# Joint first layers of a two-MoE kernel: fixed PSUM bank pairs, additions issued earlier, an earlier set of inner sums, and a third raw weight buffer

## The chip, the cores and the metric

The kernel runs on one core of a Trainium2 chip. Its time is in device microseconds (us), the median over timed executions; beside them stands one execution under the hardware profiler, from which every row below comes. Matrix products run on TensorE (PE in the rows; PEld is its weight load), element work on VectorE (DVE), ScalarE (ACT) and GpSimd (POOL); the sync engine (SP) issues the loads of the weights.

## The reference

An attention with a score threshold makes x (1152 x 512), which then passes through two mixtures of experts. Every expert is a dense two-layer network over all rows.

```python
def _moe_ref(x, w_gate, w1, w2):           # 8 experts
    ...                                    # P: gate, balanced 8 times
    for e in range(E):
        h = np.maximum(x @ w1[e], 0.0)     # 512 -> 1024
        ye = h @ w2[e]                     # 1024 -> 512
        out += P[:, e:e + 1] * ye

def _moe2_ref(x, domain_probs, w1, w2):    # 4 experts, the same form
    ...
    for e in range(E):
        h = np.maximum(x @ w1[e], 0.0)
        out += p[:, e:e + 1] * (h @ w2[e])
```

## The kernel before

**Work and stages.** After the attention (with two experts' share of rows computed behind it) the experts are run in 22 halves, each one half of an expert's 1024 inner columns. A half has a first layer (x times w1, then relu) and a second layer (times w2, added to `acc`). Every fp32 product is three fp32r products of a high and a low part: of a weight `wh` (a cast on ScalarE) and `wl` (a subtraction on GpSimd), of a hidden value `hs` high (a relu on ScalarE) and `hs` low (a scalar_tensor_tensor on VectorE, called a low part below).

**Two kinds of half.** The first layer is a Winograd form of Strassen's scheme: 7 products numbered `u` = 1 to 7 in place of 8, with sums of x and of the weights' quarters made beforehand. Six halves run it for one chunk of 576 rows at a time (`layer1`, then `layer2` of that chunk; chunk c is the first or second 576 rows). The other 16 (`TWO`: halves 3 to 12 and 16 to 21) are joint: `layer1_two` takes both chunks together, and for u = 2 and u = 7 applies the scheme once more inside; then one `layer2` goes over all 9 tiles of rows. A joint half has 162 first-layer matmuls of 288 columns (L1076) and 108 second-layer ones of 512 columns (L1279, 12 for each tile).

**Order in a joint first layer.** `ROW` is the order of TensorE's groups by hand. "a1" to "a7" are the inner products of u = 2, "b1" to "b7" those of u = 7 (3 matmuls each); "101" is u = 1, chunk 0, half of the columns 1 (6 matmuls). Copies to SBUF follow on ScalarE at once (`s`, `u`, `w` 576 wide, `A`, `B`, `C` 288 wide, tag `inner`); additions, relus and low parts are put on VectorE's and ScalarE's queues by `after(k, op)`, k slots of `ROW` later, and `done(k, ...)` is a relu after k slots and its low part one slot later. Each engine runs its queue in this order.

**Banks.** PSUM is one tile of 8 banks. `A01` are two pairs, of chunk 0 and chunk 1, for u = 1, 6, 5, 3; `X` and `Y` are pairs for the inner products of a, then again for those of b, and from there for u = 4. `ps.pair()` takes the pair that came free first, `bank()` the bank that came free first, in the program's order; `give` returns one behind the instruction that reads it last (the low part, or the addition into `acc`). The layer after waits on the chip for that reader.

**Weights.** `cook1` and `cook2` prepare units of w1 and w2: raw tiles are loaded by SP, `cook1` makes sums of quarters on GpSimd (`ws`, `wx`, in-place `raw`), and each unit is a cast and a subtraction. `tick()` places one unit at a time between the rest of the work. Of w2 two raw buffers exist (`raw2`).

**Inner sums of x.** `within_x` makes the sums of x that a and b need (24 additions or subtractions of 288 columns and low parts on VectorE, 8 casts on ScalarE) before the first joint half of each run of joint halves. It is started by `start_within()` in halves 2 and 15, and `tick` spreads it over the second layer that follows, up to 6 steps a tile.

Of the kernel before, what the change touches and what calls it, by code (L numbers as in the profile page):

```python
# [20 lines left out]
P = 128  # L21
# [9 lines left out]
def attention_two_moe_kernel(ctx, tc, qP, kP, qT, kT, vp, tau, wg, w1, w1s, w2, dp, m2w1s, m2w2, out):  # L31
# [601 lines left out]
    class Psum:  # L633
# [7 lines left out]
            self.of[id(t)] = t, (k,)  # L641
            return t

        def pair(self):
            j = min((j for j in range(4) if 2 * j in self.free and 2 * j + 1 in self.free),
                    key=lambda j: max(self.free.index(2 * j), self.free.index(2 * j + 1)))
            for k in (2 * j, 2 * j + 1):
                self.free.remove(k)
            t = self.all[:, 2 * j:2 * j + 2]
            self.of[id(t)] = t, (2 * j, 2 * j + 1)  # L650
            return t

        def give(self, t):
# [20 lines left out]
    def cook1():  # L674
# [7 lines left out]
        for i, hv in enumerate(halves):  # L682
# [20 lines left out]
                return x, clock[0] + LAG  # L703

            if i in TWO:
                yield 0, ready
                x2 = within(a12)
                yield from unit(a12, ready)
                yield from unit(*x2)
# [7 lines left out]
            yield 0, ready  # L717
            G.tensor_tensor(a21, a11, a21, op=ALU.subtract)  # L718
            s3 = a21, clock[0] + LAG
            yield from unit(*s2)  # L720
            if i in TWO:
                yield from unit(*s1)
                x7 = within(a21)
                yield from unit(*s3)
                yield from unit(*x7)
            else:
                yield from unit(*s3)
                yield from unit(*s1)
            yield 0, ready
            G.tensor_tensor(a12, a12, s2[0], op=ALU.subtract)  # L730
            yield from unit(a12, clock[0] + LAG)
            yield from unit(a22, ready)

    def cook2(w2p):
        raw = []
        todo2 = [(hv, k) for hv in halves for k in ORDER]
        for i in range(len(todo2)):
            while len(raw) < 2 and todo2:
                hv, k = todo2.pop(0)
                raw.append((w2p.tile([P, DM], F32, tag="raw2", name="raw", bufs=2), clock[0] + LAND))  # L740
                nc.sync.dma_start(raw[-1][0], hv["w2"][hv["e"], :, hv["hf"] * HF + k])
            yield i, raw[0][1]
            hi = w2p.tile([P, DM], F32R, tag="w2h", name="wh", bufs=NB2)
            lo = w2p.tile([P, DM], F32R, tag="w2l", name="wl", bufs=NB2)
            split(A, G, hi, lo, raw.pop(0)[0])
            units[1].append((hi, lo))
# [305 lines left out]
    def layer1_two(i):  # L1052
# [83 lines left out]
            after(at, go)  # L1136

        v, ps = {}, banks.pool
        A01 = [ps.pair(), ps.pair()]
        X = Y = None  # L1140
        for slot in ROW:
            if slot[0] in "ab":
                u, j = {"a": 2, "b": 7}[slot[0]], int(slot[1])
                if j == 1:
                    X, Y = ps.pair(), ps.pair()
                m = {1: X[:, 0], 6: X[:, 0], 5: X[:, 0], 3: X[:, 0], 2: Y[:, 0], 7: Y[:, 1], 4: Y[:, 1]}[j][:, :HS]
                inside(u, j, m, j in (1, 2, 7))
                if j in (1, 6, 5):
                    copy("ABC"[(1, 6, 5).index(j)], m, "inner", 3, False)
                if j == 2:  # L1150
                    after(1, lambda m=m: add(m, v["A"], m))
                if j == 5 and u == 2:
                    def far(X=X, Y=Y):
                        add(X[:, 1, :HS], v["C"], Y[:, 1, :HS])
                    after(1, far)
                if j == 5 and u == 7:
                    def far(Y=Y):
                        add(v["C"], v["C"], Y[:, 1, :HS])
                    after(1, far)
                    after(2, lambda: add(v["w1"][:, 1], v["w1"][:, 1], v["C"]))  # L1160
                    after(3, lambda: add(v["u1"][:, 1], v["u1"][:, 1], v["C"]))
                if j == 3 and u == 2:
                    after(1, lambda X=X: add(cols(X), v["s1"], cols(X)))
                    done(2, cols(X), 1, 0, 0, (X,))
                if j == 3 and u == 7:
                    after(1, lambda m=m: add(v["w1"][:, 0], v["w1"][:, 0], m))
                    done(2, v["w1"], 1, 1, 2)
                    rest(6, 1, 1)
                if j == 4:
                    after(1, lambda m=m: add(m, v["B"], m))  # L1170
                    if u == 2:
                        after(2, lambda Y=Y: add(cols(Y), v["s0"], cols(Y)))
                        done(3, cols(Y), 0, 0, 0, (Y,))
                    else:
                        after(1, lambda Y=Y: add(v["w0"], v["w0"], cols(Y)))
                        done(2, v["w0"], 0, 1, 2)
                        rest(6, 0, 1)
                if n[0] % 2:
                    tick()
# [79 lines left out]
    def layer2(i, c):  # L1259
# [10 lines left out]
            if c == hv["chunks"][-1]:  # L1270
                ts.insert(2, 8)
        for t in ts:
            py = bank()
            hs, o = (tail, 0) if t == 8 else (hv["side"][t // 4][t % 4 // 2], P * (t % 2))
            n = 0
            for j, k in enumerate(ORDER):
# [28 lines left out]
    for i, hv in enumerate(halves):  # L1305
# [4 lines left out]
        for c in hv["chunks"]:  # L1310
            layer1(i, c)
            if i == 0:
                while behind:
                    next(behind[0], None) or behind.pop(0)
                begin(0, sums(0), 2)
            if (i == 2 or i == turn + 2) and c == hv["chunks"][-1]:
                start_within()
            layer2(i, c)

# [53 lines left out]
```

## Time and profile before

| what | value |
|---|---|
| three timed runs | 1379.47, 1380.01, 1380.37 us (median 1380.01) |
| the profiled execution | 1379.62 us, span 1377.8 us from first to last instruction |
| TensorE busy | 1321.3 us of the span, mean granted clock 0.991 |
| VectorE, ScalarE, GpSimd busy | 734.2, 598.4, 814.8 us |
| one joint half (511.65 to 559.85 us) | 48.20 us |

The median lies 0.39 us above the profiled execution. TensorE is busy nearly always, so what matters is the few places where it stood still, which engine ended that, and what that engine was doing before. A busy TensorE is not one at full clock: the granted clock of a stretch says which of its two levels (1.2 and 2.4 GHz) it had.

### The profile page before, as it was taken

The page shows a single profiled execution, that of the slowest core. Times are in us where ns is not written, and L with a number is a line of the kernel's source. Part 1 is how long each engine was busy: PE and PEld are TensorE (multiplying, and loading weights), DVE is VectorE, ACT ScalarE, POOL GpSimd, SP SyncE. Part 2 cuts the span into 40 slices and gives each one's busy share as a digit, 9 for nine tenths or more (in the row PEclk, how much of TensorE's full clock was granted, in tenths as well). Part 3 has the DMA queues.
Part 4 walks back from the last instruction along what each step waited for, and adds up shares of the span by engine and source line. Part 5 has one row for each costly group of instructions (what it writes and reads, how often), then busy time and mean ns, then how long its engine had stood idle before and what let it go on. Part 6 is the DMA issues. An engine that isn't in the chain of part 4 may idle for free.

```text
span 1377.8 us, 20664 instructions
## 1 busy us (share of the span) xinstructions
PE 1321.3 (96%) x7681; PEld 1159.6 (84%) x7681; DVE 734.2 (53%) x1478; ACT 598.4 (43%) x1220; POOL 814.8 (59%) x997
## 2 busy tenths in 40 slices
PE   7998999999998999999999999999999899999998
PEld 4687988898787888898888888888788788888887
DVE  5799888266757543453454345344335645435524
ACT  6887786223433443243234324324533424333431
POOL 6886875252855755674575566455854467556540
PEclk9999999999999999999999999999999999999999
DMA  4542320010220121021011101111110101101101
GB/s 153 157 122 68 107 90 9 24 47 16 77 69 16 47 62 48 15 62 62 16 47 62 52 11 62 61 46 32 46 35 28 62 3 60 62 24 39 62 8 69
DMA packets 42051, 73.54 MB, mean 53 GB/s; under 512 B 5088, under 2 KB 10336, under 8 KB 41952
## 3 DMA queue, kind: packets, MB, share of 16 engines
q1 hardware_dynamic: 41664, 71.96, 16.8%
q8 instruction: 60, 0.98, 0.3%
q10 hardware_dynamic: 288, 0.28, 0.1%
q14 instruction: 39, 0.32, 0.1%
HBM read 69.86 MB, written 2.36 MB: 52 GB/s over the span
## 4 chain that ended last, share of the span: by engine, by line
PE 69%; DVE 12%; ACT 8%; POOL 5%; DMA 3%; issue 2%; DVEq 0%; POOLq 0%; ACTq 0%
PE mm L1279 35%; PE mm L1076 14%; PE mm L979 6%; PE mm L501 4%; PE mm L473 3%; POOL wl L77 2%; DMA raw<-in_w 2%; ACT wh L72 2%; DVE hs L1122 2%; PE pv L349 2%; PE sc L272 1%; DVE ex L296 1%; ACT hs L1118 1%; DVE acc L1287 1%; DVE st L277 1%
## 5 line engine op out<-in xcount | busy, mean ns | idle before, releaser
L77 POOL TENSOR_TENSOR wl<-raw,wh 128x512 fp32r<-128x512 f32 x198 | 261.7, 1328 | 336.1 <-ACT wh L72 333.6
L1279 PE MATMUL mm<-wh,hs 128*128 128x512 f32 x1344 | 432.7, 395 | 2.5 <-DVE hs L952 2.4
L1279 PEld LDWEIGHTS mm<-wh,hs 128*128 128x128 f32 x1344 | 252.4, 188 | 65.5 <-DVE hs L952 6.6
L1279 PE MATMUL mm<-wl,hs 128*128 128x512 f32 x672 | 265.3, 395 | 1.6 <-POOL wl L77 1.6
L1287 DVE SCALAR_TENSOR_TENSOR acc<-mm,p,acc 128x512 f32<-128x512 f32 x181 | 133.8, 748 | 244.8 <-PE mm L1279 244.6
L72 ACT CAST wh<-raw 128x512 fp32r<-128x512 f32 x198 | 122.4, 622 | 73.5 <-POOL raw L718 33.1
L1279 PEld LDWEIGHTS mm<-wl,hs 128*128 128x128 f32 x672 | 126.3, 188 | 30.2 <-POOL wl L77 2.3
L1076 PE MATMUL mm<-xh,wl 128*128 128x288 f32 x432 | 99.8, 304 | 18.5 <-DVE acc L1287 18.4
L1122 DVE SCALAR_TENSOR_TENSOR hs<-mm,hs 128x576 fp32r<-128x576 f32 x96 | 72.5, 755 | 68.8 <-ACT hs L1118 65.8
L1118 ACT ACTIVATE hs<-mm 128x576 fp32r<-128x576 f32 x96 | 62.4, 650 | 82.3 <-DVE mm L1115 81.5
L1076 PE MATMUL mm<-xl,wh 128*128 128x288 f32 x432 | 97.5, 298 | 0.0
L1076 PE MATMUL mm<-xh,wh 128*128 128x288 f32 x432 | 97.0, 297 | 0.0
L1076 PEld LDWEIGHTS mm<-xh,wl 128*128 128x128 f32 x432 | 72.0, 192 | 23.5 <-DVE acc L1287 22.8
L1112 ACT COPY A<-mm 128x288 f32<-128x288 f32 x32 | 13.1, 408 | 171.5 <-PE mm L1076 171.5
L1076 PE MATMUL mm<-xth,wl 128*128 128x288 f32 x304 | 71.1, 302 | 9.7 <-DVE hs L1122 9.3
L1134 POOL TENSOR_SCALAR ht<-hs 128x128 fp32r<-128x128 f32 x128 | 44.3, 359 | 48.8 <-ACT hs L1118 32.9
L1076 PEld LDWEIGHTS mm<-xl,wh 128*128 128x128 f32 x432 | 72.1, 192 | 0.7
L1076 PEld LDWEIGHTS mm<-xh,wh 128*128 128x128 f32 x432 | 72.0, 192 | 0.0
L306 POOL TENSOR_SCALAR ex<-ex,st 128x576 f32<-128x576 f32 x72 | 54.1, 752 | 26.6 <-DVE st L304 23.6
L1076 PE MATMUL mm<-xth,wh 128*128 128x288 f32 x304 | 68.9, 295 | 0.0
L1076 PE MATMUL mm<-xtl,wh 128*128 128x288 f32 x304 | 68.8, 295 | 0.0
L296 DVE SCALAR_TENSOR_TENSOR ex<-sc,st,ex 128x576 f32<-128x576 f32 x72 | 58.5, 813 | 14.8 <-ACT ex L292 11.0
(220 smaller groups left out, 3002.0 us busy)
## 6 DMA issues: line engine op xcount, KB each, us to landing
raw<-in_w SPq DMA_DIRECT2D x88, 256.0 KB, 2.9
raw<-in_w1s SPq DMA_DIRECT2D x56, 256.0 KB, 3.7
raw<-in_m2w1s SPq DMA_DIRECT2D x32, 256.0 KB, 3.5
raw<-in_m2w SPq DMA_DIRECT2D x32, 256.0 KB, 2.9
kr<-in_kT SPq DMA_DIRECT2D x22, 288.0 KB, 2.8
vr<-in_vp SPq DMA_DIRECT2D x24, 160.0 KB, 2.4
qr<-in_qT SPq DMA_DIRECT2D x8, 288.0 KB, 2.8
out_y<-acc SPq DMA_DIRECT2D x8, 256.0 KB, 2.0
```

The lines of the kernel that those rows point to most:

```text
L72: A.copy(hi, src)
L77: el.tensor_tensor(lo, src, f(hi), op=ALU.subtract)
L296: V.scalar_tensor_tensor(ex, u["sc"][:, :, :HS], st[:, 2:3], ex, op0=ALU.is_ge, op1=ALU.mult, accum_out=st[:, 3:4])
L306: G.tensor_scalar(exf, exf, st[:, 5:6], 1.0, op0=ALU.mult, op1=ALU.mult)
L501: T.matmul(py, lhsT=x, rhs=a, start=i == 0, stop=i == 3 * FT - 1)
L979: T.matmul(m, lhsT=w[:, (2 * g + kt) * P:(2 * g + kt + 1) * P], rhs=operand(u, kt, lo), start=first and j == 0, stop=j == len(ops) - 1, sk ...
L1076: T.matmul(m, lhsT=w, rhs=x, start=first and j == 0, stop=last and j == len(ops) - 1, skip_group_check=True)
L1118: A.activation(sides[c][s][0][:, k:k + 2], src, AF.Relu)
L1122: V.scalar_tensor_tensor(hl, src, 0.0, f(hh), op0=ALU.max, op1=ALU.subtract)
L1134: G.tensor_scalar(tail[j][:, :, q:q + 32], f(sides[c][s][j][:, :, 2 * P:]), 1.0, 1.0, op0=ALU.mult, op1=ALU.mult)
L1279: T.matmul(py, lhsT=hs[x][:, k, o:o + P], rhs=w, start=n == 0, stop=n == 3 * HF - 1)
L1287: V.scalar_tensor_tensor(acc[t], py, s, acc[t], op0=ALU.mult, op1=ALU.add)
```

## The change

It touches the joint halves (their banks, their order on VectorE and ScalarE), the order of `cook1` in all halves, the number of raw w2 buffers, and the place where `within_x` starts.

- Banks: `A01` is always banks 0, 1 and 2, 3; `X` is 4, 5 and `Y` 6, 7, both for a and for b. The second layer of a joint half uses banks 2 and 3 by turns in place of all eight.
- `after` and `done` have smaller k: an addition goes on the queue in the slot of the product that it waits for.
- `inner` copies have 2 buffers in place of 3, raw w2 tiles 3 in place of 2.
- `cook1` makes the subtraction for its second to last unit (`s4`) before the units s2, s1, s3, and in joint halves the sums `x7` as well; the first sums `x2` get a start LAG later.
- `start_within()` stands behind the first layer of the half's first chunk, not of its last.

```diff
-        def pair(self):
-            j = min((j for j in range(4) if 2 * j in self.free and 2 * j + 1 in self.free),
-                    key=lambda j: max(self.free.index(2 * j), self.free.index(2 * j + 1)))
-            for k in (2 * j, 2 * j + 1):
+        def take(self, *ks):
+            for k in ks:
                 self.free.remove(k)
...
             if i in TWO:
-                yield 0, ready
+                yield 0, ready + LAG
                 x2 = within(a12)
...
-            yield from unit(*s2)
-            if i in TWO:
-                yield from unit(*s1)
-                x7 = within(a21)
-                yield from unit(*s3)
-                yield from unit(*x7)
-            else:
-                yield from unit(*s3)
-                yield from unit(*s1)
             yield 0, ready
             G.tensor_tensor(a12, a12, s2[0], op=ALU.subtract)
-            yield from unit(a12, clock[0] + LAG)
+            s4 = a12, clock[0] + LAG
+            if i in TWO:
+                yield 0, ready
+                x7 = within(a21)
+                rest = s2, s1, s3, x7, s4
+            else:
+                rest = s2, s3, s1, s4
+            for src in rest:
+                yield from unit(*src)
...
-            while len(raw) < 2 and todo2:
+            while len(raw) < 3 and todo2:
...
-        A01 = [ps.pair(), ps.pair()]
+        A01 = [ps.take(0, 1), ps.take(2, 3)]
...
-                    X, Y = ps.pair(), ps.pair()
+                    X, Y = ps.take(4, 5), ps.take(6, 7)
...
-                    copy("ABC"[(1, 6, 5).index(j)], m, "inner", 3, False)
+                    copy("ABC"[(1, 6, 5).index(j)], m, "inner", 2, False)
...
                 if j == 3 and u == 2:
-                    after(1, lambda X=X: add(cols(X), v["s1"], cols(X)))
-                    done(2, cols(X), 1, 0, 0, (X,))
+                    after(0, lambda X=X: add(cols(X), v["s1"], cols(X)))
+                    done(1, cols(X), 1, 0, 0, (X,))
                 if j == 3 and u == 7:
-                    after(1, lambda m=m: add(v["w1"][:, 0], v["w1"][:, 0], m))
-                    done(2, v["w1"], 1, 1, 2)
+                    after(0, lambda m=m: add(v["w1"][:, 0], v["w1"][:, 0], m))
+                    done(1, v["w1"], 1, 1, 2)
                     rest(6, 1, 1)
                 if j == 4:
-                    after(1, lambda m=m: add(m, v["B"], m))
+                    after(0, lambda m=m: add(m, v["B"], m))
                     if u == 2:
-                        after(2, lambda Y=Y: add(cols(Y), v["s0"], cols(Y)))
-                        done(3, cols(Y), 0, 0, 0, (Y,))
+                        after(0, lambda Y=Y: add(cols(Y), v["s0"], cols(Y)))
+                        done(1, cols(Y), 0, 0, 0, (Y,))
                     else:
-                        after(1, lambda Y=Y: add(v["w0"], v["w0"], cols(Y)))
-                        done(2, v["w0"], 0, 1, 2)
+                        after(0, lambda Y=Y: add(v["w0"], v["w0"], cols(Y)))
+                        done(1, v["w0"], 0, 1, 2)
                         rest(6, 0, 1)
...
-            py = bank()
+            py = banks.pool.take(2 + ts.index(t) % 2) if i in TWO else bank()
...
-            if (i == 2 or i == turn + 2) and c == hv["chunks"][-1]:
+            if (i == 2 or i == turn + 2) and c == hv["chunks"][0]:
                 start_within()
```

The order on ScalarE in the middle of a joint first layer, from the copy `s` of chunk 0 to the copy `w` of chunk 0, before:

```order
L1112 COPY s_5781<-mm 128x576
L1112 COPY C<-mm 128x288
L72 CAST wh<-raw 128x512
L1112 COPY s_5809<-mm 128x576
L72 CAST wh<-raw 128x512
L1112 COPY u_5837<-mm 128x576
L72 CAST wh<-raw 128x512
L1118 ACTIVATE hs<-mm 128x576
L1112 COPY u_5859<-mm 128x576
L72 CAST wh<-raw 128x512
L1118 ACTIVATE hs<-mm 128x576
L1112 COPY w_5887<-mm 128x576
```

and of the change:

```order
L1109 COPY s_5783<-mm 128x576
L72 CAST wh<-raw 128x512
L1109 COPY C<-mm 128x288
L72 CAST wh<-raw 128x512
L1109 COPY s_5818<-mm 128x576
L1115 ACTIVATE hs<-mm 128x576
L1109 COPY u_5842<-mm 128x576
L72 CAST wh<-raw 128x512
L1115 ACTIVATE hs<-mm 128x576
L1109 COPY u_5863<-mm 128x576
L72 CAST wh<-raw 128x512
L1109 COPY w_5889<-mm 128x576
```

The fourth cast of w2 (the second cast of the rows, before as of the change) now stands ahead of the second `s`, and the relu of `X` follows that copy directly, where a cast, a copy and a cast stood between them.

The order on VectorE from the addition of `C` of b to the last low part of the w's, near the end of the joint first layer (`w_5887` is chunk 0, `w_5915` chunk 1), before:

```order
L1115 TENSOR_TENSOR C<-C,mm 128x288
L1115 TENSOR_TENSOR w_5915<-w_5915,C 128x288
L1122 SCALAR_TENSOR_TENSOR hs<-mm,hs 128x576
L1115 TENSOR_TENSOR u_5859<-u_5859,C 128x288
L1115 TENSOR_TENSOR w_5915<-w_5915,mm 128x288
L1115 TENSOR_TENSOR mm<-B,mm 128x288
L1115 TENSOR_TENSOR w_5887<-w_5887,mm 128x576
L1122 SCALAR_TENSOR_TENSOR hs<-w_5915,hs 128x576
L1122 SCALAR_TENSOR_TENSOR hs<-mm,hs 128x576
L1122 SCALAR_TENSOR_TENSOR hs<-w_5887,hs 128x576
```

and of the change (`w_5889` is chunk 0, `w_5917` chunk 1):

```order
L1112 TENSOR_TENSOR C<-C,mm 128x288
L1112 TENSOR_TENSOR w_5917<-w_5917,C 128x288
L1119 SCALAR_TENSOR_TENSOR hs<-mm,hs 128x576
L1112 TENSOR_TENSOR u_5863<-u_5863,C 128x288
L1112 TENSOR_TENSOR w_5917<-w_5917,mm 128x288
L1112 TENSOR_TENSOR mm<-B,mm 128x288
L1112 TENSOR_TENSOR w_5889<-w_5889,mm 128x576
L1119 SCALAR_TENSOR_TENSOR hs<-w_5917,hs 128x576
L1119 SCALAR_TENSOR_TENSOR hs<-w_5889,hs 128x576
L1119 SCALAR_TENSOR_TENSOR hs<-mm,hs 128x576
```

The second `hs<-mm`, the low part that gives back the pair of chunk 1 (now banks 2 and 3), has moved from second to last place among the three low parts.

## Rows read from the trace of the kernel before

**Rows 1.** The page, busy time of each engine with its share of the span.

```profile
PE 1321.3 (96%) x7681; PEld 1159.6 (84%) x7681; DVE 734.2 (53%) x1478; ACT 598.4 (43%) x1220; POOL 814.8 (59%) x997
```

**Rows 2.** TensorE's waits: waiting line, releaser, us in total, times, longest.

```profile
PE mm L1076 <- DVE acc L1287: 18.4, 16, 6.1
PE mm L1076 <- DVE hs L1122: 9.3, 16, 1.0
...
PE mm L1279 <- POOL wl L77: 1.6, 2, 1.4
```

**Rows 3.** Windows, second and first layer: us; busy PE, PEld, DVE, ACT, POOL; granted clock.

```profile
511.65:536.80 25.15, 25.15 (x110) 20.33 (x110) 9.99 (x15) 4.09 (x7) 13.93 (x20) 1.00 0.00 1
536.80:559.85 23.05, 22.03 (x163) 21.56 (x162) 11.16 (x18) 13.55 (x26) 14.75 (x14) 1.00 0.31 92
```

**Rows 4.** Timeline of TensorE in one joint first layer: start, us, idle before.

```profile
488.36 0.29 PE L1076 MATMUL mm<-xh,wl 128*128 128x288 f32 x1
...
489.36 0.40 PE L1076 MATMUL mm<-xh,wl 128*128 128x288 f32 x1 [0.45 <-DVE acc L1287]
...
500.77 0.42 PE L1076 MATMUL mm<-xh,wh 128*128 128x288 f32 x2
...
501.81 0.40 PE L1076 MATMUL mm<-xth,wl 128*128 128x288 f32 x1 [0.62 <-DVE hs L1122]
...
511.49 0.40 PE L1279 MATMUL mm<-wh,hs 128*128 128x512 f32 x1
```

**Rows 5.** The chain of waits that ends at 501.81.

```profile
493.58 2.83 DMA raw<-in_w
...
500.24 0.66 ACT hs L1118
...
501.00 0.77 DVE hs L1122
```

**Rows 6.** Timeline of VectorE from b's `C` to the next second layer.

```profile
505.74 0.46 DVE L1115 TENSOR_TENSOR C<-C,mm 128x288 f32<-128x288 f32 x1 [2.71 <-ACT C L1112]
...
509.60 1.57 DVE L1122 SCALAR_TENSOR_TENSOR hs<-w,hs 128x576 fp32r<-128x576 f32 x1
511.10 0.74 DVE L1122 SCALAR_TENSOR_TENSOR hs<-mm,hs 128x576 fp32r<-128x576 f32 x1
511.76 1.18 DVE L1122 SCALAR_TENSOR_TENSOR hs<-w,hs 128x576 fp32r<-128x576 f32 x1
...
517.16 1.40 DVE L1287 SCALAR_TENSOR_TENSOR acc<-mm,p,acc 128x512 f32<-128x512 f32 x2
```

**Rows 7.** Timeline of GpSimd in the same stretch.

```profile
503.13 0.46 POOL L702 TENSOR_TENSOR wx<-raw 128x128 f32<-128x128 f32 x1 [2.05 <-DMA raw<-in_w1s]
...
510.64 1.70 POOL L679 TENSOR_TENSOR ws<-ws,raw 128x512 f32<-128x512 f32 x1
```

**Rows 8.** Timeline of VectorE, inner sums of x, in two places.

```profile
421.54 3.85 DVE L1034 TENSOR_TENSOR sums<-xh,xl 128x288 f32<-128x288 f32 x4
...
433.44 1.55 DVE L1034 TENSOR_TENSOR sums<-xth,xtl 128x288 f32<-128x288 f32 x4
```

**Rows 9.** Windows: the wait of the first joint half, and its first 12 matmuls.

```profile
433.40:439.56 6.16, 0.04 (x1) 0.00 (x1) 6.09 (x16) 1.53 (x4) 0.00 (x0) 0.68 0.00 0
439.56:442.56 3.00, 3.00 (x12) 3.00 (x13) 1.07 (x2) 0.92 (x2) 0.88 (x1) 0.51 0.00 0
```

**Rows 10.** Timeline of TensorE, the same wait in half 16.

```profile
1083.81 0.61 PE L1076 MATMUL mm<-xh,wl 128*128 128x288 f32 x1 [5.99 <-DVE acc L1287]
```

**Rows 11.** Timeline of VectorE, then of GpSimd, half 2's first second layer.

```profile
398.25 0.46 DVE L952 SCALAR_TENSOR_TENSOR hs<-mm,hs 128x288 fp32r<-128x288 f32 x1 [0.48 <-ACT hs L951]
...
402.25 0.75 DVE L1287 SCALAR_TENSOR_TENSOR acc<-mm,p,acc 128x512 f32<-128x512 f32 x1 [2.04 <-PE mm L1279]
...
410.25 0.46 DVE L994 TENSOR_TENSOR mm<-s,mm 128x288 f32<-128x288 f32 x1 [1.69 <-PE mm L979]
...
410.38 1.29 POOL L77 TENSOR_TENSOR wl<-raw,wh 128x512 fp32r<-128x512 f32 x1 [11.30 <-ACT wh L72]
```

More of the change, by code (lines that the diff above doesn't have):

```diff
@@ L642, in tile @@
             return t
-        def pair(self):
-            j = min((j for j in range(4) if 2 * j in self.free and 2 * j + 1 in self.free),
-                    key=lambda j: max(self.free.index(2 * j), self.free.index(2 * j + 1)))
-            for k in (2 * j, 2 * j + 1):
+        def take(self, *ks):
+            for k in ks:
                 self.free.remove(k)
-            t = self.all[:, 2 * j:2 * j + 2]
-            self.of[id(t)] = t, (2 * j, 2 * j + 1)
+            t = self.all[:, ks[0]] if len(ks) == 1 else self.all[:, ks[0]:ks[1] + 1]
+            self.of[id(t)] = t, ks
             return t
@@ L737, in cook2 @@
         for i in range(len(todo2)):
-            while len(raw) < 2 and todo2:
+            while len(raw) < 3 and todo2:
                 hv, k = todo2.pop(0)
-                raw.append((w2p.tile([P, DM], F32, tag="raw2", name="raw", bufs=2), clock[0] + LAND))
+                raw.append((w2p.tile([P, DM], F32, tag="raw2", name="raw", bufs=3), clock[0] + LAND))
                 nc.sync.dma_start(raw[-1][0], hv["w2"][hv["e"], :, hv["hf"] * HF + k])
@@ L1148, in layer1_two @@
                 if j in (1, 6, 5):
-                    copy("ABC"[(1, 6, 5).index(j)], m, "inner", 3, False)
+                    copy("ABC"[(1, 6, 5).index(j)], m, "inner", 2, False)
                 if j == 2:
-                    after(1, lambda m=m: add(m, v["A"], m))
+                    after(0, lambda m=m: add(m, v["A"], m))
                 if j == 5 and u == 2:
@@ L1154, in far @@
                         add(X[:, 1, :HS], v["C"], Y[:, 1, :HS])
-                    after(1, far)
+                    after(0, far)
                 if j == 5 and u == 7:
@@ L1158, in far @@
                         add(v["C"], v["C"], Y[:, 1, :HS])
-                    after(1, far)
+                    after(0, far)
                     after(2, lambda: add(v["w1"][:, 1], v["w1"][:, 1], v["C"]))
```

## The prediction

> **What bounds the kernel now.** I read the busy times first, then TensorE's waits, then the joint halves stage by stage, then the timeline around each wait. TensorE is busy 1321.3 of 1377.8 us [rows 1], so only the 56 us in which it stands still, and what they entail, can be won. The list of its waits shows where half of them lie: in the joint first layers it waits 18.4 us for an `acc` addition (16 times) and 9.3 us for a low part (16 times) [rows 2]. Sixteen is the number of joint halves: each has one wait of either kind.
>
> A joint half repeats in 48.20 us [rows 3]. Its second layer runs without a gap: 9 tiles in 25.15 us, 2.79 us a tile. Its first layer takes 23.05 us, while 162 matmuls at 0.133 us (the last 72 take 501.81 to 511.49 us [rows 4]) need 21.55. The missing 1.5 us are two stalls:
>
> - Stall A, at "a2". The 3 matmuls of "a1" start at 488.36 and need 0.40 us, the next starts only at 489.36 [rows 4]: 0.60 us lost, and 0.1 more because the first matmul behind a pause takes 0.40 where 0.29 is usual. It waits for the `acc` addition of the last tile, whose bank had become `Y`.
> - Stall B, at "b2". After 500.77 the two matmuls need 0.27 us, the next starts at 501.81: 0.77 lost, and again 0.1. The profile shows 0.62 of it as idle [rows 4]. The bank is a's `Y`, given back by a low part at 501.00 [rows 5]. Followed back, that low part stands behind a relu at 500.24, this behind an addition, and that behind the low part of `X`; and all of it behind a cast on ScalarE that waited for a load of raw w2, 493.58 + 2.83 = 496.41 us [rows 5].
>
> In the first joint half of each run stall A is of another size: 6.12 and 5.99 us [rows 9, 10], because VectorE was busy 6.09 of 6.16 us [rows 9], with the inner sums and the `acc` additions queued behind them. Then comes a second price: the first 12 matmuls take 3.00 us at a granted clock of 0.51, the 1.2 GHz level, in place of 12 x 0.133 = 1.6 [rows 9].
>
> **What each part changes, and its price.**
>
> 1. *Stall A, 14 usual ones.* "a2" now writes bank 6. The second layer writes only 2 and 3, and 6 was given back at its beginning. The idle time of the 14 is 18.4 - 6.12 - 5.99 = 6.3 us [rows 2, 9, 10]; each costs 0.6 + 0.1 where 0.45 is shown, so 14 x 0.27 = 3.8 more. Gain 10.1. Bank 2 is needed next at "110", 3.2 us into the layer, long after the last tile's addition (0.75 us, [rows 11]).
>
> 2. *Stall B, 16.* With three raw buffers the load for the fourth w2 cast starts behind the first subtraction in place of the second, about 2.9 us into the layer, and lands at 5.75 (duration of [rows 5]). The relu of `X` follows its addition at once, and `Y`'s addition goes ahead of `X`'s low part. Step by step from the layer's start (a group of 6 takes 0.8 us, results are seen 0.2 later): copy of the second `s` 6.3 to 6.9, addition of `X` to 7.7, relu to 8.4, a copy and a cast to 9.5, relu of `Y` to 10.2, its low part to 10.95. "b2" wants the bank at 12.0: 1 us to spare. The cover is this slack; without it the stall is back. Gain 9.3 + 16 x 0.27 = 13.6.
>
> 3. *Inner sums.* They move to the second layer of the first chunk, two stages earlier. There VectorE idles 2.04 us of each 2.79 us tile [rows 11] and GpSimd 11.30 us in one piece [rows 11]. That matters: four sums took 3.85 us while GpSimd worked and 1.55 while it rested [rows 8]. At the second pace 8 additions, 8 subtractions and 8 low parts, 24 x 0.4, are 10 us, with four `acc` additions of 0.75 almost 13, from 398.7 (the first layer's last low part) to 411.4 us. VectorE's next work began at 410.25 [rows 11], so it starts 1.2 us late. Queued behind are that first layer's additions and, on ScalarE behind 8 casts, its copies `s`; TensorE wants the first `s` read 3.2 us into that layer, and by this count it is, with 1 us to spare. I take no cost; the bound is the old pace throughout, 24 x 0.96 = 23 us in place of 10, some 5 to 10 us too late for that layer each time, of which a later stall would bring back up to 5. Gain (6.12 + 5.99) + 2 x 0.16 + 2 x 1.4 of slow clock = 15.2, at least 5.
>
> 4. *A new wait at the second layer's start.* The second layer begins in bank 2, which chunk 1's low part gives back, and this now stands last of three low parts on VectorE. Before, b's `C` went in 5.75 us ahead of the second layer (505.74 against 511.49), and the chain from there ran without a pause to 512.94, 1.45 us behind that start [rows 6]. Its length is partly GpSimd's doing: low parts with an SBUF source took 1.57 and 1.18 us, one from PSUM 0.74 [rows 6], while GpSimd worked from 503.13 to 512.3 [rows 7]. With the new order GpSimd has only the `wx` sums until then: the cast for the next subtraction stands behind the relu of chunk 1 on ScalarE, and the `ws` sums behind the tails. So I price the chain without contention: the two additions with `C` as before and, behind its relu, chunk 0's low part from 4.7 to 4.0 us ahead of the start, three additions of 0.4 to 2.8, `w0` (576 wide) to 2.1, the low part of `w1` to 1.4, that of `w0` behind its relu from 1.3 to 0.6, and chunk 1's with its 0.74 [rows 6] until 0.16 behind the start. The price is 0.2 + 0.1 = 0.3 us a half, 16 x 0.3 = 4.8. The bounds: nothing, if it is 0.2 faster; and, if the chain keeps its old length with the two low parts exchanged, 512.94 + 0.74 - 511.49 = 2.2 us, with 0.1 for the restart 16 x 2.3 = 37. I take the lower one, since the work that made the old rows long is queued later.
>
> 5. *Two banks in the second layer.* A tile needs 2.79 us, its addition 0.75 [rows 3, 11], so with turns a bank is free 2 us before it is wanted. The exception is the first: its addition came at 517.16 [rows 6], while the third tile would want its bank at 511.49 + 2 x 2.79 = 517.07, and the addition ends near 517.9. In the new order the chain of step 4 is about 1.2 us shorter, the addition ends near 516.6, and the tile wants the bank at 517.3. Cost nothing, bound 16 x 0.8 = 13.
>
>    The Trainium skill, page "Perfetto Trace Analysis" (section "Matmul Optimizations"), speaks against this edit: it asks that all 8 banks be put to use. By it the second layer would lose time, which the last rival prices; by the rows the sum stays as it is, since 0.75 is less than 2.79.
>
> 6. *The rest.* The third buffer places one cast of the first half earlier, where TensorE waits 1.6 us for GpSimd's subtraction [rows 2]; between 0 and 3 with its restarts, I take 1. The order in `cook1` moves one subtraction of about 1.3 us ahead of the units; in a second layer GpSimd is busy 13.93 of 25.15 us [rows 3], which leaves room. Two `inner` buffers: each copy comes after the addition that read its buffer two copies ago. Nothing for both.
>
> Sum: 10.1 + 13.6 + 15.2 + 1 - 4.8 = 35.1 us. The profiled execution took 1379.62, so 1344.5; the median of the runs is 0.4 above its own profile, which gives **1345**.
>
> **Rivals.**
>
> - *The low parts stay slow* (chance 0.2). GpSimd still works in the last 3 us of the first layer, for example because the loads for `wx` land late (they landed at 503.13 [rows 7], 8.4 us before the end). Then step 4 costs between 1 and 2 us a half, or step 5 its 0.8: 1354 to 1370. For it: [rows 6] as they are. Against: the order on ScalarE.
> - *The sums only move their stall* (0.08). If GpSimd's work falls on them, TensorE waits at the copies of half 2 and half 15: up to 10 us less gain, 1349 to 1355.
> - *The new wait takes everything* (0.03 slower, 0.04 no change). The place is bank 2 at the start of the second layer. Step 4 without its price gains 39.9 us, so from 39.9 / 16 = 2.5 us a half the kernel is slower. The old chain with the low parts exchanged gives 2.3, which is 1376.5; 0.2 us more contention and it is no gain. It needs GpSimd as busy as in [rows 7], with all three low parts at 1.57.
> - *The wait of B stays* (0.04), if the load of the fourth raw tile lands over 1 us later than I reckon: 13.6 less, 1358.
> - *Two banks bind every tile* (0.01). If no addition overlapped the next tiles, each of the 144 joint tiles would wait 0.8 us, 115 us in all: 1460. It would need additions 2 us late, tile after tile; [rows 11] show them in 0.75 with 2.04 of rest. The skill's rule on banks, named in step 5, is this case.
>
> **How the numbers follow.** My forecast, 1340 to 1349, has the remaining 0.6. The rivals of 1349 to 1362 take in some 0.2 more; below 1340 lies only the case that step 4 costs nothing. So the range is 1338 to 1362. Changes under 0.2% (2.8 us) can't be told from none. Faster 0.92, within it 0.04, slower 0.04.
>
> **What would show it.** Right: a joint half of 46.9 to 47.1 us; no wait of TensorE for `acc` in the joint first layers; 16 short waits at L1276 for the last low part; the sums uncontended, near 0.39 us each; a granted clock of 1.0 in the first matmuls of halves 3 and 16. Wrong: idle time over 0.5 us before the first or the third second-layer tile, low parts from SBUF above 1 us, or TensorE waiting at L976 in halves 2 and 15.

## The result, and the profile after

The changed kernel took **1343.45 us** (median of 4 runs, 1342.15 to 1344.37), the kernel before in the same session 1379.74 (1378.57 to 1380.37): ratio 0.9737, 95% interval 0.972 to 0.9754. Forecast: 1345, range 1338 to 1362. Line numbers behind the weights' code moved up by three: L1076 is now L1073, L1279 is L1276, L1122 is L1119.

The page of the changed kernel, busy time (beside [rows 1]):

```profile
PE 1311.2 (98%) x7681; PEld 1156.2 (86%) x7681; DVE 706.0 (53%) x1478; ACT 600.9 (45%) x1220; POOL 788.4 (59%) x997
```

The span fell from 1377.8 to 1341.1 us. TensorE's waits, of which [rows 2] showed 18.4 us for `acc` and 9.3 for a low part:

```profile
PE mm L976 <- ACT u L983: 2.1, 2, 1.9
...
PE mm L976 <- ACT w L983: 1.4, 2, 0.8
...
PE mm L976 <- ACT s L983: 0.9, 1, 0.9
...
PE mm L1276 <- DVE hs L1119: 0.3, 1, 0.3
```

Both large lines are gone. In the joint halves the list names one wait, 0.3 us. The waits for copies of ScalarE in the first layers of other halves (L976) have grown to 4.4 us; before there was one, 0.7 us for a `w`. A joint half, second and first layer (windows, beside [rows 3]), and the first matmuls of halves 3 and 16 (beside [rows 9]):

```profile
500.64:525.84 25.20, 25.20 (x109) 20.39 (x110) 8.71 (x12) 4.25 (x8) 17.31 (x23) 1.00 0.00 1
525.84:547.56 21.72, 21.69 (x164) 21.45 (x162) 11.12 (x20) 13.67 (x26) 9.84 (x11) 1.00 0.31 97
432.02:433.62 1.60, 1.60 (x14) 1.59 (x13) 1.22 (x2) 0.92 (x2) 0.01 (x1) 1.00 0.00 0
1055.66:1057.26 1.60, 1.60 (x14) 1.59 (x13) 1.22 (x2) 0.92 (x2) 0.01 (x1) 1.00 0.00 0
```

46.92 us in place of 48.20; and the first joint halves start at a granted clock of 1.00 where 0.51 stood.

Where the 36.7 us of span came from, read from the first matmul of each stretch (for half 3 before, 433.27, the turn of its first matmul, which stalled):

| stretch | before | after | gained | forecast |
|---|---|---|---|---|
| up to half 0 (code that the change doesn't touch) | 331.17 | 329.65 | 1.5 | 0 |
| halves 0 to 2 | 102.10 | 102.37 | -0.3 | 1 |
| half 3 and half 16, the first joint ones | 55.09, 55.42 | 46.91, 46.90 | 16.7 | 16.3 |
| 14 other joint halves | 434.79, 245.22 | 422.65, 238.54 | 18.8 | 17.8 |
| halves 13 to 15 | 154.01 | 154.08 | -0.1 | 0 |

The forecasts of the joint halves are the terms of the text: 15.2 + 2 x (0.85 - 0.3) for the first ones, 14 x (0.72 + 0.85 - 0.3) for the others. The first row is scatter: in the profiles below half 0 begins anywhere from 329.73 to 331.53.

**The new wait.** TensorE at the second layer's start, and VectorE before it (timelines of the changed kernel):

```profile
500.19 0.42 PE L1073 MATMUL mm<-xth,wh 128*128 128x288 f32 x2
500.64 0.50 PE L1276 MATMUL mm<-wh,hs 128*128 128x512 f32 x1
500.98 0.39 PE L1276 MATMUL mm<-wl,hs 128*128 128x512 f32 x1
```

```profile
494.71 0.46 DVE L1112 TENSOR_TENSOR C<-C,mm 128x288 f32<-128x288 f32 x1 [2.71 <-ACT C L1109]
...
498.32 1.59 DVE L1119 SCALAR_TENSOR_TENSOR hs<-w,hs 128x576 fp32r<-128x576 f32 x2
499.84 0.75 DVE L1119 SCALAR_TENSOR_TENSOR hs<-mm,hs 128x576 fp32r<-128x576 f32 x1
```

Two matmuls from 500.19 need 0.27, so the next was due at 500.46 and came at 500.64, when the low part that gives bank 2 back ends (499.84 + 0.75 = 500.59); and it is followed after 0.34 where 0.23 is usual. 0.18 + 0.1 = 0.28 us: the forecast said 0.3. The low parts of the `w` took 0.8 us each, not the 1.57 and 1.18 of [rows 6], and GpSimd stood still beside them, for 7.27 us up to its next subtraction:

```profile
500.25 1.29 POOL L77 TENSOR_TENSOR wl<-raw,wh 128x512 fp32r<-128x512 f32 x1 [7.27 <-ACT wh L72]
```

**The sums** (VectorE in half 2; beside [rows 8, 11]):

```profile
397.28 1.65 DVE L1031 TENSOR_TENSOR sums<-xh,xl 128x288 f32<-128x288 f32 x4
...
407.21 1.56 DVE L77 TENSOR_TENSOR xi<-sums,tails 128x288 fp32r<-128x288 f32 x4
408.69 0.74 DVE L1284 SCALAR_TENSOR_TENSOR acc<-mm,p,acc 128x512 f32<-128x512 f32 x1
409.35 0.83 DVE L991 TENSOR_TENSOR mm<-s,mm 128x288 f32<-128x288 f32 x2
```

0.4 us each, and VectorE reaches the next first layer's work 3.05 us into it (406.30 to 409.35) where it was 2.65 before: 0.4 us late (the forecast said 1.2), and nothing waits.

**What came back.** The third buffer takes 3.1 us off half 0's second layer (17.30 to 14.23), and half 1's first layer gets 3.5 longer (11.39 to 14.85). TensorE, a window of what follows its wait, VectorE and GpSimd of the changed kernel there:

```profile
364.34 0.53 PE L976 MATMUL mm<-xh,wl 128*128 128x288 f32 x2 [1.91 <-ACT u L983]
```

```profile
364.97:368.25 3.28, 3.28 (x16) 3.28 (x15) 1.79 (x5) 1.66 (x4) 3.20 (x4) 0.51 0.30 80
```

```profile
356.41 2.36 DVE L857 TENSOR_TENSOR sums<-xh,xl 128x288 f32<-128x288 f32 x2
358.69 1.55 DVE L861 TENSOR_TENSOR sums<-sums 128x288 f32<-128x288 f32 x1
...
362.59 0.81 DVE L991 TENSOR_TENSOR mm<-s,mm 128x288 f32<-128x288 f32 x2
```

```profile
352.53 7.39 POOL L77 TENSOR_TENSOR wl<-raw,wh 128x512 fp32r<-128x512 f32 x5
```

While GpSimd works until 359.92, an addition of two SBUF tiles takes VectorE 1.2 to 1.5 us. So the additions to `s` start only at 362.59, behind them waits a relu, behind that the copy `u`, and for that TensorE, 1.9 us. The matmuls behind the wait run at a granted clock of 0.51 for 3.3 us, which costs the rest.

### The profile page after: what moved, and what is told of

Its sections match the earlier page's. It is cut to its first block, busy times and chain, and to the rows that moved or that the text cites. A ratio compares the mean times of both kernels' runs of the same rounds, so it can differ in the third digit from the quotient of the medians.

```text
span 1341.1 us, 20708 instructions
## 1 busy us (share of the span) xinstructions
PE 1311.2 (98%) x7681; PEld 1156.2 (86%) x7681; DVE 706.0 (53%) x1478; ACT 600.9 (45%) x1220; POOL 788.4 (59%) x997
## 4 chain that ended last, share of the span: by engine, by line
PE 85%; DVE 7%; ACT 4%; POOL 3%; issue 1%; DMA 0%; POOLq 0%; DVEq 0%; ACTq 0%
PE mm L1276 38%; PE mm L1073 25%; PE mm L976 6%; PE mm L501 5%; PE mm L473 3%; PE sc L272 2%; PE pv L349 2%; DVE ex L296 1%; PE et L314 1%; DVE st L277 1%; ACT ex L292 1%; PE pv L358 1%; DVE etl L331 1%; PE pv L356 1%; DVE sums L857 1%
## 5 line engine op out<-in xcount | busy, mean ns | idle before, releaser
L77 POOL TENSOR_TENSOR wl<-raw,wh 128x512 fp32r<-128x512 f32 x198 | 256.9, 1304 | 383.2 <-ACT wh L72 377.2
L1276 PE MATMUL mm<-wh,hs 128*128 128x512 f32 x1344 | 433.4, 397 | 2.4 <-DVE hs L949 1.6
L1276 PEld LDWEIGHTS mm<-wh,hs 128*128 128x128 f32 x1344 | 252.3, 188 | 67.7 <-DVE hs L1119 4.5
L1276 PE MATMUL mm<-wl,hs 128*128 128x512 f32 x672 | 265.1, 394 | 0.0
L1276 PEld LDWEIGHTS mm<-wl,hs 128*128 128x128 f32 x672 | 126.3, 188 | 28.2
L1073 PE MATMUL mm<-xh,wl 128*128 128x288 f32 x432 | 96.6, 296 | 0.0
L1073 PE MATMUL mm<-xl,wh 128*128 128x288 f32 x432 | 96.4, 295 | 0.0
L1073 PE MATMUL mm<-xh,wh 128*128 128x288 f32 x432 | 96.2, 295 | 0.0
L1119 DVE SCALAR_TENSOR_TENSOR hs<-mm,hs 128x576 fp32r<-128x576 f32 x96 | 72.5, 755 | 33.7 <-ACT hs L1115 32.2
L1073 PEld LDWEIGHTS mm<-xh,wl 128*128 128x128 f32 x432 | 70.7, 189 | 0.8
L1073 PEld LDWEIGHTS mm<-xl,wh 128*128 128x128 f32 x432 | 70.7, 188 | 0.8
L1073 PEld LDWEIGHTS mm<-xh,wh 128*128 128x128 f32 x432 | 71.0, 189 | 0.0
L1073 PE MATMUL mm<-xth,wl 128*128 128x288 f32 x304 | 69.0, 296 | 0.0
L1073 PE MATMUL mm<-xth,wh 128*128 128x288 f32 x304 | 68.9, 295 | 0.0
L1073 PE MATMUL mm<-xtl,wh 128*128 128x288 f32 x304 | 68.8, 295 | 0.0
L1276 PE MATMUL mm<-wh,ht 128*128 128x512 f32 x176 | 58.2, 392 | 1.8 <-POOL ht L957 1.8
```

Of the source, the lines that this page charges most:

```text
L77: el.tensor_tensor(lo, src, f(hi), op=ALU.subtract)
L1073: T.matmul(m, lhsT=w, rhs=x, start=first and j == 0, stop=last and j == len(ops) - 1, skip_group_check=True)
L1119: V.scalar_tensor_tensor(hl, src, 0.0, f(hh), op0=ALU.max, op1=ALU.subtract)
L1276: T.matmul(py, lhsT=hs[x][:, k, o:o + P], rhs=w, start=n == 0, stop=n == 3 * HF - 1)
```

## The experiments

Twelve kernels. Each ratio is to the kernel before, run beside it; joint halves in us, from first layer to first layer, without half 12, which has plain halves behind it and differs in most runs.

| run | us | ratio to before, 95% interval | joint half |
|---|---|---|---|
| the changed kernel | 1343.45 | 0.9737 (0.972 to 0.9754) | 46.91 |
| pairs_that_came_free_first | 1350.04 | 0.9782 (0.9767 to 0.9797) | 47.32 |
| additions_one_slot_later | 1352.52 | 0.9797 (0.978 to 0.9813) | 47.50 |
| sums_in_the_last_chunk_again | 1360.28 | 0.9857 (0.9842 to 0.9871) | 46.90 |
| two_raw_buffers | 1346.23 | 0.9755 (0.9741 to 0.977) | 46.9 to 47.3 |
| second_layer_in_banks_1_and_0 | 1338.05 | 0.9706 (0.9692 to 0.9719) | 46.61 |
| second_layer_in_four_banks | 1343.21 | 0.9742 (0.9729 to 0.9755) | 46.91 |
| low_part_of_chunk_1_second_again | 1341.66 | 0.973 (0.9716 to 0.9743) | 46.74 |
| weight_order_as_before | 1384.65 | 1.0038 (1.0026 to 1.0051) | 48.9 or 50.4 |
| first_wx_sums_without_the_delay | 1384.56 | 1.0033 (1.0022 to 1.0044) | 48.9 or 50.4 |
| delay_of_the_first_wx_sums_alone | 1379.59 | 0.9997 (0.9987 to 1.0006) | 48.2 |
| no_delay_and_banks_1_and_0 | 1361.67 | 0.9866 (0.9852 to 0.9881) | 48.27 |
| banks_1_and_0_and_slower_sums | 1335.31 | 0.9677 (0.9663 to 0.9692) | 46.61 |

**The banks undone** (pairs_that_came_free_first):

```diff
-        A01 = [ps.take(0, 1), ps.take(2, 3)]
+        A01 = [ps.pair(), ps.pair()]
...
-                    X, Y = ps.take(4, 5), ps.take(6, 7)
+                    X, Y = ps.pair(), ps.pair()
...
-            py = banks.pool.take(2 + ts.index(t) % 2) if i in TWO else bank()
+            py = bank()
```

> The changed kernel with the old choice of banks in the joint halves (the pair and the bank that came free first), all else as changed. Here Y of a is again the bank of the last tile before. Theory (fixed banks took stall A away, at the price of the new wait for bank 2): 14 to 16 stalls of 0.7 us at the group a2 are back, 10 to 11.5 us, and the 0.28 us at the second layer's start that the changed profile shows 16 times (4.5 us) is gone: about 1349.5 us, joint halves of 47.3 us. Rival (the banks changed nothing, the additions issued earlier took A away): joint halves of 46.65 us, 1339. Rival (all eight banks help the second layer more than that): below 1343.

TensorE's waits of that run:

```profile
PE mm L1078 <- DVE acc L1289: 7.2, 16, 0.5
```

Stall A is back in all 16, and the second layer is 25.09 in place of 25.19 us, since it no longer waits for bank 2. As the theory: the fixed banks took one stall away and brought a smaller one.

**The additions undone** (additions_one_slot_later): `after(0)` and `done(1)` of the joint halves back to the old slots, `inner` at two buffers.

> The changed kernel with the additions, relus and low parts of the joint first layers in their old slots; banks, third raw buffer (and two inner buffers), sums and weight order as changed. Theory: the order is needed against stall B. The low part of Y then ends some 1.5 us later than now, where the changed profile shows 1.2 us to spare, so 0.3 to 0.5 us of stall are back 16 times, 5 to 8 us; the low part of chunk 1 goes back to second place, which returns the 0.28 us at the second layer's start, 4.5 us: 1344 to 1347 in all. Rival (the third buffer alone removed B, the order did nothing for it): no stall at b2, and 4.5 us less than the changed kernel, 1339. Rival (the order alone did it): the whole 13.6 us back, 1352 to 1357.

TensorE's waits, and its timeline at "b2":

```profile
PE mm L1073 <- DVE hs L1119: 7.8, 16, 0.5
```

```profile
492.51 0.42 PE L1073 MATMUL mm<-xh,wh 128*128 128x288 f32 x2
493.43 0.40 PE L1073 MATMUL mm<-xth,wl 128*128 128x288 f32 x1 [0.50 <-DVE hs L1119]
```

Stall B is back, but larger than the theory gave it, and the time is that of the last rival (the order alone did it, 1352 to 1357): the low part of `Y` ends 1.9 us later than in the changed kernel (12.56 against 10.68 us into the layer), not 1.5, and some 0.65 + 0.1 us are lost 16 times. The first layer takes 22.29 us where 21.52 is the time without any wait: 0.77 x 16 = 12.3 of the 13.6 us of the forecast's step 2 hang on the order alone. Nor did all of the new wait's price come back: the second layer still took 25.20, now because its third tile loses 0.11 us behind the first addition.

**The sums undone** (sums_in_the_last_chunk_again):

```diff
-            if (i == 2 or i == turn + 2) and c == hv["chunks"][0]:
+            if (i == 2 or i == turn + 2) and c == hv["chunks"][-1]:
```

> The changed kernel with the inner sums of x begun behind the first layer of the last chunk again. Theory (VectorE is still busy with the sums when the joint half begins): TensorE waits 5 to 6 us at a2 of halves 3 and 16 and then runs 12 matmuls at the 1.2 GHz level, 1.4 us, together 13 to 15 us: about 1358. Rival (with fixed banks or with GpSimd's work elsewhere the sums end in time in the old place too): waits under 1 us there and less than 3 us in all, 1343 to 1346.

TensorE's waits of that run:

```profile
PE mm L1073 <- DVE acc L1284: 10.8, 2, 5.6
```

The theory: fixed banks don't help where VectorE itself is late. 16.8 us more than the changed kernel.

**Two raw buffers** (two_raw_buffers): `bufs=3` and `len(raw) < 3` back to 2.

> The changed kernel with two raw w2 buffers. Theory (the order of the additions has enough slack without the third buffer): the low part of Y ends about 0.6 us later than now, still before b2 wants its bank, the joint halves stay at 46.9 us; half 0 loses the 3 us that it gained at its second layer, and the 3.5 us that the changed profile lost one first layer later (the wait for the copy u at 362 us and the slow matmuls behind it) come back: 1343 to 1346. Rival (the third buffer is what removed stall B): 0.5 to 0.85 us at b2 in all 16 joint halves, 8 to 14 us: 1352 to 1357.

No wait at "b2"; the low part of `Y` ends 10.85 us into the layer, 0.17 later than with three. So my step 2, which made the third buffer the start of the chain, gave it a part that it doesn't need. Half 0's second layer is back at 17.71 us and half 1's first layer at 11.16: halves 0 to 2 take 102.14 us, with three buffers 102.37. What the buffer is worth lies in the joint halves, 2.6 us (471.31 and 286.30 us for the two runs of them, against 469.56 and 285.44), and the two medians are 2.8 apart, about the least that can be told. A third of it is half 12, which takes 48.2 us and waits before its second layer; most of the rest are steps up to 0.3 us too long at the start of group "500", whose bank the copy `u` of chunk 0 has to read first (in half 8 that copy ends at 677.21 and the matmul starts at 677.35, 0.15 late). The wait in half 12:

```profile
PE mm L1276 <- DVE hs L1119: 1.0, 1, 1.0
```

**Other banks for the second layer** (second_layer_in_banks_1_and_0 and second_layer_in_four_banks):

```diff
-            py = banks.pool.take(2 + ts.index(t) % 2) if i in TWO else bank()
+            py = banks.pool.take(1 - ts.index(t) % 2) if i in TWO else bank()
```

```diff
+            py = banks.pool.take((1, 0, 3, 2)[(ts.index(t) - 1) % 4]) if i in TWO else bank()
```

> The changed kernel with the second layer of a joint half in banks 1 and 0 by turns (1 first) in place of 2 and 3. Bank 1 is given back by the low part of chunk 0, which the changed profile shows 4 us ahead of the second layer (495.76 + 0.76 against 500.64). Theory (the 0.28 us between the last first-layer matmul and the rhythm of the second layer is the wait for bank 2 and its restart): joint halves of 46.65 us in place of 46.91, 16 x 0.27 = 4.3 us less than the changed kernel, about 1339. Rival (the 0.28 us is the price of a new layer's first matmuls whatever the bank, or the wait comes back at the group 100 of the next half): 1342 to 1345.

> The changed kernel with the second layer of a joint half in four banks by turns (2, 1, 0, 3, ...), still 2 first. Theory (a bank is free 2 us before it is wanted, two banks cost nothing): 46.91 us a joint half, 1342 to 1345 as the changed kernel. Rival (two banks hold the second layer up, and the 0.1 us that it is longer than before is their price): second layers of 25.09 in place of 25.19 us, 1.6 us or more less: below 1342.

Windows of the first of them, second and first layer:

```profile
501.45:526.54 25.09, 25.09 (x111) 20.29 (x110) 8.90 (x13) 4.44 (x8) 17.52 (x23) 1.00 0.00 1
526.54:548.06 21.52, 21.52 (x164) 21.52 (x162) 10.93 (x19) 13.51 (x26) 9.67 (x11) 1.00 0.32 98
```

Joint halves of 46.61 us, 0.30 less, in all 16: the new wait is gone, and TensorE has no idle time left in a joint half. Four banks that begin with 2 change nothing: it matters which bank comes first, not how many there are. The Trainium skill, page "Perfetto Trace Analysis" (section "Matmul Optimizations"), asks for all 8; in this kernel two that are free in time take 25.09 us for a second layer, and so do eight by turns in the run with the old pairs. That run's longer half (47.32 against 46.61) is stall A at "a2". Eight banks with fixed pairs were not run.

**The low parts' order** (low_part_of_chunk_1_second_again):

```diff
-                        done(1, v["w0"], 0, 1, 2)
+                        done(2, v["w0"], 0, 1, 2)
```

> The changed kernel with the relu and low part of w0 a slot later, so that the low part that gives back banks 2 and 3 stands second of the three again. Theory: the bank is free 0.75 us earlier, before TensorE wants it; joint halves of 46.65 us, about 1339 as with banks 1 and 0. Rival (the 0.28 us is no wait for this low part): 46.91 us, 1342 to 1345. Rival (the low part of w0 as the last one comes too late for the second layer, or the first addition for the third tile): a new gap inside the second layer, 0.1 to 0.8 us, 1341 to 1352.

Between the theory and its last rival: the first layer falls to 21.52, but the second takes 25.22, since the third tile now loses 0.13 us to a wait for its bank (in half 12 long enough for the timeline to name it):

```profile
882.05 0.50 PE L1276 MATMUL mm<-wh,hs 128*128 128x512 f32 x1 [0.17 <-DVE acc L1284]
```

By its time alone it can't be told from the changed kernel.

**The order of the weights undone** (weight_order_as_before), and of it one word (first_wx_sums_without_the_delay):

```diff
             if i in TWO:
-                yield 0, ready + LAG
+                yield 0, ready
                 x2 = within(a12)
```

> The changed kernel with the units of cook1 in their old order (the subtraction for the fourth unit and the sums x7 back behind the units). Theory: the new order put two ws sums ahead of the x sums on GpSimd in half 14, so that the casts of ScalarE and the copies behind them came late there (waits of TensorE at 958.54 to 968.86, with restarts 3.1 us, of which 0.8 stood before too); the old order takes 2.3 us off: 1341. In the joint halves nothing changes. Rival (the new order keeps GpSimd quiet while the low parts run at the end of the joint first layer): low parts of 1.2 to 1.6 us there, a wait of 1 to 2 us before the second layer, 1355 or more. Rival: no difference, 1343.

> The changed kernel with one word undone: the first sums x2 of cook1 get their start at ready in place of ready + LAG; the rest of the order of cook1 stays as changed. Theory (this delay is what keeps GpSimd quiet beside the last low parts): ScalarE's next two w1 casts stand ahead of the relus of w1 and w0 again, GpSimd's two subtractions fall on the additions and low parts, which end 2 us later, and TensorE waits 2.0 us for bank 2 in 15 or 16 joint halves: 1380 to 1387, like the run with the whole old order of the weights (1384.65). Rival (it is the order of the other units, the early fourth subtraction and x7, that does it): 1341 to 1346.

The first theory fell: not 2.3 us faster but 41 slower, slower than the kernel before; its rival, which I had not believed, is what happened. The waits in half 14 stay (0.8 us for `s`, 1.4 for `w`), so the order of the weights isn't their cause. With two raw buffers the second of the two waits for `w` is absent, as it was before:

```profile
PE mm L976 <- ACT w L983: 0.7, 1, 0.7
```

The last second layer of half 13 and the first layer behind it take 32.8 to 33.0 us together in the three kernels with two raw buffers, and 33.7 to 34.1 in the eleven with three: the third buffer has a price here too, as in half 1. What decides the wait for `s` stays open.

The run with one word undone shows that this word does all of it. Its waits, then TensorE, VectorE, ScalarE and GpSimd in one half, and windows of 4 us behind two of the pauses:

```profile
PE mm L1276 <- DVE hs L1119: 28.5, 15, 2.0
```

```profile
503.79 0.42 PE L1073 MATMUL mm<-xth,wh 128*128 128x288 f32 x2
506.23 0.50 PE L1276 MATMUL mm<-wh,hs 128*128 128x512 f32 x1 [2.02 <-DVE hs L1119]
```

```profile
502.17 3.33 DVE L1119 SCALAR_TENSOR_TENSOR hs<-w,hs 128x576 fp32r<-128x576 f32 x2
505.43 0.74 DVE L1119 SCALAR_TENSOR_TENSOR hs<-mm,hs 128x576 fp32r<-128x576 f32 x1
```

```profile
498.18 0.62 ACT L72 CAST wh<-raw 128x512 fp32r<-128x512 f32 x1
...
499.24 0.62 ACT L72 CAST wh<-wx 128x512 fp32r<-128x512 f32 x1
501.19 0.69 ACT L1115 ACTIVATE hs<-w 128x576 fp32r<-128x576 f32 x1 [1.33 <-DVE w L1112]
```

```profile
498.88 1.54 POOL L77 TENSOR_TENSOR wl<-raw,wh 128x512 fp32r<-128x512 f32 x1 [2.03 <-ACT wh L72]
500.38 1.51 POOL L77 TENSOR_TENSOR wl<-wx,wh 128x512 fp32r<-128x512 f32 x1
501.85 1.30 POOL L677 TENSOR_TENSOR ws<-raw 128x512 f32<-128x512 f32 x1
503.22 1.67 POOL L677 TENSOR_TENSOR ws<-ws,raw 128x512 f32<-128x512 f32 x1
```

```profile
457.35:461.40 4.05, 4.05 (x17) 3.30 (x18) 2.62 (x4) 1.91 (x4) 1.71 (x6) 1.00 0.00 0
506.23:510.30 4.07, 4.07 (x12) 3.19 (x13) 2.63 (x4) 1.93 (x4) 1.71 (x6) 0.62 0.00 0
```

Without the delay ScalarE casts the next two units ahead of the relus, GpSimd works without a pause from 498.88 until behind the low parts of the `w`, and the two low parts of the `w` take 1.67 us each in place of 0.8. TensorE waits 2.0 us in 14 of the 16 halves, and behind 8 of these pauses its granted clock falls, to 0.58 to 0.68 over the next 4 us (0.62 in the last row; the one above it is a pause without that), so that those second layers take 26.73 in place of 25.19 us. 14 x 1.98 + 8 x 1.54 = 40 us; measured 41. The low part from PSUM keeps its 0.74 us. The Trainium skill, page "SBUF — State Buffer" (section "Who interferes with whom"), says that a VectorE instruction with two SBUF inputs contends with GpSimd's reads of SBUF, and that one with at most one SBUF input does not (modes that use two ports apart); these rows agree, 1.67 against 0.74.

**The delay by itself** (delay_of_the_first_wx_sums_alone): the same word, put into the kernel before.

> The kernel before with this one word of the change: x2 a start LAG later. Theory: in the kernel before nothing waits for the last low parts (its second layer begins in a bank that came free long before), so a quieter GpSimd there gives nothing; stalls A and B stay, joint halves of 48.2 us, 1377 to 1382. Rival (the slow low parts also cost the kernel before time): 2 us or more faster in each joint half, below 1350.

1379.59 against 1379.89: nothing, as the theory. The word is worth 41 us in the changed kernel, where a bank hangs on the last low part, and none in the kernel before, where nothing does.

**No delay, and a bank that is free** (no_delay_and_banks_1_and_0), both edits above together:

> The changed kernel without that delay, and with the second layer in banks 1 and 0. The low parts are as late as without the delay (they end about 2.1 us after the last first-layer matmul's turn), but no bank is waited for. Theory (of the 2.2 us a half most was the bank, and what stays is the operand: the first tile wants chunk 1's last low part with its 7th matmul, 1.4 us into the second layer): 0.7 to 0.9 us a half, 1350 to 1355 with some slow matmuls behind the pauses. Rival (the wait was for the operand all along): 2 us a half stay, 1375 to 1385. Rival (it was the bank alone): 1338 to 1341.

TensorE in one second layer:

```profile
504.05 0.50 PE L1276 MATMUL mm<-wh,hs 128*128 128x512 f32 x1 [0.66 <-DVE hs L1119]
...
509.00 0.50 PE L1276 MATMUL mm<-wh,hs 128*128 128x512 f32 x1 [0.49 <-DVE acc L1284]
```

The wait for the operand is what the theory gave, 0.8 us, 0.9 with the restart. It had forgotten the next one: the `acc` addition of the first tile stands behind the same late low parts, and the third tile waits for its bank, 0.65 us, 0.75 with the restart. Together 1.66 us a half, 23.6 in the medians, so the time is 7 us above the theory's range. This is where two banks do cost something: only once the low parts are late.

**A faster version** (banks_1_and_0_and_slower_sums):

```diff
-                begin(0, sums(0), 2)
+                begin(0, sums(0), 3)
```

> The second layer in banks 1 and 0, and the sums of x for chunk 0 spread over three ticks each in place of two (5 of VectorE's additions move from half 0's second layer to half 1's). Theory (the wait of 2 us for the copy u at 362 us in the changed kernel, and the slow matmuls behind it, come from VectorE, whose additions of two SBUF tiles take 1.2 to 1.5 us while GpSimd works): with 5 of them less ahead, 2 to 3.5 us less than with banks 1 and 0 alone, 1334.5 to 1336.5. Rival (the copies are late for another reason, or the sums moved are late one half on): 1337 to 1340.

1335.31 us. Half 1's first layer takes 11.15 us in place of 14.86, without a wait: it was VectorE's queue, as the theory has it. This is the fastest kernel of the study, 8 us below the changed one.

## Why the prediction was right, and where it was not

- *Stall A, 10.1 us, and stall B, 13.6 us*: shown by undoing the banks and the additions; each brought its stall back in all 16 halves, A with 0.71 and B with 0.77 us. (The 0.27 that both sums add for each stall is 0.25 by their own terms, 0.6 us in all.) The mechanism of B was half right: the additions' order was enough, the earlier load of the fourth raw tile was not needed.
- *Sums, 15.2 us*: shown; 16.8 when undone, and the pace of 0.4 us an addition that I had assumed from [rows 8] was the measured one.
- *The new wait, 0.3 us a half*: 0.28 by the timeline and 0.30 by the run in banks 1 and 0.
- *Two banks, nothing*: shown by four banks, 1343.21. Its exception, the third tile, has no slack when anything ahead of it is late (it loses 0.11 to 0.75 us in three runs).
- *The step that failed is 6.* For the third buffer I took 1 us in half 0; there it won 3.1 and lost 3.5, and its 2.6 us lie in the joint halves. For the order in `cook1` I wrote "Nothing for both". The change to that order carries 41 us: step 4 rests on a quiet GpSimd, which I read from the new order of the queues without asking which edit makes it. It is the `LAG` of the first sums. The condition was right and the sum came out; but whoever had taken step 6 at its word and left that edit out would have made the kernel slower than before. My upper bound for the new wait, 2.3 us a half, is close to what that kernel shows (2.17 + 0.1, and the slow clock behind it on top), but by luck. The bound adds 0.74 us to a chain whose end, 512.94, already holds all three low parts; in the new order the old lengths give 1.45 + 0.1 (and the rival that rests on the bound 1364.5 in place of 1376.5). The missing 0.7 came from low parts slower than in [rows 6]: the three take 4.0 us there, before 3.3.
- *Not undone by itself*: the two `inner` buffers. That they cost nothing is read from rows, not from a run: in half 4 of the changed kernel the copies `A`, `B` and `C` wait on ScalarE for TensorE or for nothing.

- *What would show it*: the joint half of 46.9, the sums at 0.4, the clock of 1.00 and the missing `acc` waits came as written. Of the 16 short waits the list names one, 0.3 us in half 12; the others, 0.18 us, show only in the step between the rows. TensorE waits at L976 not in halves 2 and 15, where I looked for it, but in 1 and 14.

The profiled execution took 1343.3 us, 1.2 below the sum of 1344.5; the untouched stretch ahead of half 0 was 1.5 shorter.

## What to carry to other kernels

When a wait is traded for another one, find out what keeps the new one short, down to the edit that does it, and cost that edit by what happens without it: a word that was worth nothing in the kernel before held 41 us here. When banks are fixed by hand, begin with the one whose last reader is furthest ahead; how many there are matters less. Work moved earlier on GpSimd can be paid for by VectorE's additions of two SBUF tiles (in half 1, 0.45 us each while GpSimd rested and 1.2 to 1.5 while it worked), so look at what VectorE owes next.

## What was not expected of the hardware

Of 14 pauses of the same 2.0 us at the same place in the joint half (first_wx_sums_without_the_delay), 8 were followed by matmuls at the 1.2 GHz level (granted clock 0.58 to 0.68 over the next 4 us) and 6 by none; busy times of VectorE, ScalarE and GpSimd in these windows are the same. The run weight_order_as_before has the same 14 pauses, and again 8 of them were followed by slow matmuls. In the run with neither delay nor wait for a bank, pauses of 0.66 and 0.49 us in one second layer left no slow matmuls in any of the 14 second layers that have them. What decides it stays open.
